# A mixed MLP and segment-attention kernel on one core: V computed first, transposes moved to DMA, speculation spread through the MLP, attention in a hand-set TensorE order

## The chip, the cores and the metric

One core of one Trainium2 chip. The metric is the device time of one execution in microseconds, the median of several runs. The kernel before took 1676.1 us here (4 runs, 1675.5 to 1676.5).

## The reference, cut to what matters

```python
def reference(...):                                  # bf16 inputs, S = 2048 tokens, D = 1024
    xn = layernorm(A_x)
    return A_x + A(xn) + B(xn)

def A(x):                                            # 64 segments of 32 tokens, 32 heads of 128
    mem = mem0                                       # 8 rows
    for s in range(64):
        h = concat([mem, x[segment s]])              # 40 rows
        q, k, v = h @ Wq, h @ Wk, h @ Wv             # 1024 -> 4096 each
        p = softmax(where(mask, q @ k.T * scale, -1e9))
        o = (p @ v) @ Wo
        mem = o[:8];  outs.append(o[8:])

def B(x):                                            # token-shift MLP
    h  = gelu(layernorm(x) @ w1)                     # 1024 -> 1024
    x1 = x + shift(h) @ w2                           # four channel groups shifted by -1, +1, -2, +2 tokens
    return x1 + gelu(layernorm(x1) @ w3) @ w4        # 1024 -> 3584 -> 1024
```

The recurrence over `mem` is broken by speculation: both kernels guess every segment's memory rows from averages (71 rows in all), run all segments in parallel with the guesses, and verify them at the end. If the check fails, a serial fallback runs.

## The kernel before: the parts that matter

The stages are: first stage (normalise the tokens, transpose them, `w1`, GELU), stage two (`w2`, residual, second norm, transpose), the MLP (`w3`, GELU, `w4`, four token blocks of 512), the speculation in one piece before the last `w4` chain, then attention in blocks of 12 segments with the output projection after each block. A scheduler decides the order of instructions on each engine.

```python
# first stage, for each of 16 token tiles: 8 identity matmuls for xn2, 8 "spread" matmuls for xn
nc.tensor.matmul(ps[:, k, :], xn2[:, (k0 + k) * P:(k0 + k + 1) * P], ident[:], start=True, stop=True)
nc.tensor.matmul(ps[:, k, :], xn[:, (k0 + k) * P:(k0 + k + 1) * P], spread[:], start=True, stop=True)   # 132 columns
...
# attention, for each block and each of 8 groups of 4 heads
for B, QT in zip(Bs, QTs):
    proj_T(B, wq, QT, QSCALE)            # 32 matmuls, 396 columns
for B, KTt in zip(Bs, KTs):
    proj_T(B, wk, KTt, None)             # 32 matmuls, 396 columns
for B, V in zip(Bs, Vs):
    proj_V(B, wv, V, cs_)                # 24 matmuls of 512 columns, then small DMAs put V in place
for B, QT, KTt, V in zip(Bs, QTs, KTs, Vs):
    attention(B, hg, QT, KTt, V)
...
# inside attention(): one tile = 3 segments with their memory rows, T = 99 rows, 4 heads at once
nc.tensor.matmul(S3[:, hh, :], QT[:, hh, l0:l0 + T], KTt[:, hh, l0:l0 + T], start=True, stop=True)      # scores
nc.vector.tensor_tensor(sm[:T, :, :T], S3, msk..., op=ALU.add)
nc.vector.tensor_reduce(mx[:T, :], sm[:T, :, :T], axis=AX.X, op=ALU.max)
nc.vector.tensor_tensor(sm[:T, :, :T], sm[:T, :, :T], mx..., op=ALU.subtract)
nc.scalar.activation(e[:T, :, :T], sm[:T, :, :T], ACTF.Exp, scale=LN2)
nc.vector.tensor_reduce(ss[:T, :], e[:T, :, :T], axis=AX.X, op=ALU.add)
nc.vector.reciprocal(rs[:T, :], ss[:T, :])
nc.vector.tensor_tensor(Pn[:T, :, :T], e[:T, :, :T], rs..., op=ALU.mult)
nc.tensor.matmul(T3[:, hh, :], Pn[:T, hh, :T], ident[:T, :T], start=True, stop=True)                    # transpose
nc.scalar.copy(PT[:T, :, :T], T3)
nc.tensor.matmul(O3[:, hh, :], V[:T, ti, hh * P:(hh + 1) * P], PT[:T, hh, :T], start=True, stop=True)   # outputs
...
# memory rows: 71 rows are the stationary side, 512 columns move (speculation, their V, verification)
nc.tensor.matmul(psz[ch][:NQ, :], vbT[:, h, :], wo[:, hh, ch * 512:(ch + 1) * 512], ...)
```

## Time and profile before

The page of the kernel before: its span, the busy time of the engines, and, in 40 equal slices of the span, the busy share of TensorE (PE) and the clock granted to it, in tenths. PEld are TensorE's weight loads, DVE is VectorE, ACT ScalarE, POOL GpSimd; SP, further down, is SyncE, which issues most of the DMAs here.

```profile
span 1674.9 us, 26877 instructions
PE 1626.2 (97%) x10393; PEld 863.9 (52%) x10513; DVE 647.2 (39%) x1528; ACT 640.6 (38%) x1321; POOL 220.9 (13%) x380
PE   6999999999999999999999999999999999999998
PEclk9999999999999999999999999999999999999999
```

TensorE is busy nearly always and at full clock, while every other engine is idle for more than half the time. Busy time alone does not say whether TensorE could be faster: matmuls are pipelined, so the cost of one is better read from start to start. In steady state these steps were 216 ns for 512 columns, 168 for 396, 58 for 132, 56 for 128, 47 for 99 and 35 for 71. Multiplied by the counts in the program they give a **floor**: the time that TensorE would need if it never waited. For this kernel it is 1572 us. The other 103 us I call the excess.

Four of the eleven lines of the list of TensorE's waits of the kernel before (what waited, for what: us in total, times, longest):

```profile
PE ps L233 <- ACT xn_160 L223: 10.9, 1, 10.9
PE ps L241 <- DVE xn2T L235: 5.4, 2, 4.3
PE psT L483 <- DVE Pn L479: 4.3, 14, 0.9
PE ps L147 <- DMA wv<-in_A_Wv_dram: 2.6, 3, 1.4
```

It holds few long waits after the start. The rest of the excess is in small pieces. The timeline of TensorE inside attention (start, duration, line, tiles, count) shows them:

```profile
1018.80 0.33 PE L419 MATMUL ps<-hTb,wk 128*128 128x396 bf16 x1
1019.10 0.34 PE L489 MATMUL psO<-PT,V_9567 99*128 99x99 bf16 x4
1019.43 0.39 PE L483 MATMUL psT<-c_ident_sb,Pn 99*99 99x99 bf16 x4
1019.66 1.01 PE L419 MATMUL ps<-hTb,wk 128*128 128x396 bf16 x5
1020.50 0.34 PE L489 MATMUL psO<-PT,V_9567 99*128 99x99 bf16 x4
```

Outputs (L489) and transposes (L483) stand one or two groups behind what they depend on, so many of them start 0.1 to 0.2 us late (in these rows the output at 1019.10 and the transpose at 1019.43). A group of heads takes 19.4 us against a floor of 18.1.

By stage (rows: window, its length, then busy time and instructions of PE, PEld, DVE, ACT and POOL, granted clock, DMA share, GB/s):

```profile
11.00:94.00 83.00, 76.16 (x634) 49.77 (x642) 45.16 (x122) 56.92 (x111) 22.98 (x36) 1.00 0.69 259
94.00:163.00 69.00, 64.44 (x361) 30.77 (x367) 48.66 (x107) 33.49 (x44) 21.22 (x32) 0.98 0.60 206
163.00:579.00 416.00, 410.81 (x2106) 191.99 (x2145) 32.92 (x61) 71.94 (x120) 39.26 (x31) 1.00 0.35 119
579.00:1669.00 1090.00, 1074.69 (x7295) 591.31 (x7360) 512.37 (x1215) 475.58 (x1045) 130.92 (x265) 1.00 0.49 151
```

The rows are the first stage, stage two, the MLP with the speculation, and attention with V.

### The profile page before, as it was taken

Reading aid. Unit: us, or ns where it says so; the run is one execution under the profiler, and the core shown is the slowest. Engines: PE = TensorE matmul, PEld = TensorE weight load, DVE = VectorE, ACT = ScalarE, POOL = GpSimd, SP = SyncE. Lnnn points to the kernel's source line nnn. Section 1 sums busy time; section 2 is a strip of 40 time slices with the busy share of each in tenths; the row PEclk is TensorE's granted clock in tenths of the full one; section 3 lists DMA queues with packets and bytes.
Section 4 is the critical chain, followed back from the end, with each engine's and each line's share of the span. In section 5 each row is a group of like instructions: output and inputs, shape, how many; then the busy total and the mean of one; then the engine's idle time right before and its main releaser. Section 6 shows DMA issues by size and latency. Waiting matters only on the chain.

```text
span 1674.9 us, 26877 instructions
## 1 busy us (share of the span) xinstructions
PE 1626.2 (97%) x10393; PEld 863.9 (52%) x10513; DVE 647.2 (39%) x1528; ACT 640.6 (38%) x1321; POOL 220.9 (13%) x380
## 2 busy tenths in 40 slices
PE   6999999999999999999999999999999999999998
PEld 5544444444445455554555545554555546665643
DVE  8447000000101145552455505564255533465540
ACT  7635302112030044541455415553255514565520
POOL 4222011010200122220111101110011100101000
PEclk9999999999999999999999999999999999999999
DMA  6864421030309887552565526564365633445211
GB/s 243 327 201 166 176 65 62 32 95 1 120 7 341 301 293 244 175 173 72 178 189 178 165 86 194 178 190 141 116 193 172 183 95 118 138 129 152 65 45 46
DMA packets 202804, 252.95 MB, mean 151 GB/s; under 512 B 15691, under 2 KB 165400, under 8 KB 202672
## 3 DMA queue, kind: packets, MB, share of 16 engines
q1 hardware_dynamic: 186928, 217.25, 41.1%
q0 software_dynamic: 15744, 33.92, 5.7%
q8 instruction: 85, 1.39, 0.3%
q14 instruction: 47, 0.39, 0.1%
HBM read 204.11 MB, written 30.07 MB: 140 GB/s over the span
## 4 chain that ended last, share of the span: by engine, by line
PE 75%; DVE 10%; ACT 5%; DMA 4%; issue 3%; POOL 0%; SPq 0%; DVEq 0%; ACTq 0%; POOLq 0%
PE ps L419 16%; PE ps L431 13%; PE ps L317 11%; PE ps L362 11%; PE ps L338 11%; DVE Pn L479 3%; DVE ss L475 2%; PE psT L483 2%; PE psO L489 2%; PE ps L256 2%; ACT e L473 2%; PE psS L466 2%; DMA wv<-in_A_Wv_dram 1%; DVE sm L471 1%; DVE sm L468 1%
## 5 line engine op out<-in xcount | busy, mean ns | idle before, releaser
L419 PE MATMUL ps<-hTb,wk 128*128 128x396 bf16 (+2 forms) x1536 | 265.7, 313 | 0.0
L419 PE MATMUL ps<-hTb,wq 128*128 128x396 bf16 (+2 forms) x1536 | 263.5, 314 | 0.8 <-DVE Ro L339 0.8
L362 PE MATMUL ps<-wo_sb,oX 128*128 128x512 bf16 x998 | 226.4, 379 | 1.2
L431 PE MATMUL ps<-wv,xTb 128*128 128x512 bf16 x984 | 224.4, 379 | 2.1
L338 PE MATMUL ps<-w_sb,h3T 128*128 128x512 bf16 x876 | 194.9, 379 | 1.1
L317 PE MATMUL ps<-xn3T,w_sb 128*128 128x512 bf16 x876 | 193.3, 379 | 1.1
L468 DVE TENSOR_TENSOR sm<-psS,c_mask_reg_sb 99x396 f32<-99x396 f32 x160 | 87.4, 563 | 218.1 <-PE psS L466 218.1
L419 PEld LDWEIGHTS <-wq 128*128 128x128 bf16 x1536 | 133.7, 98 | 71.3 <-issue 1.1
L318 ACT ACTIVATE h3T<-ps 128x512 bf16<-128x512 f32 x112 | 66.6, 597 | 268.1 <-PE ps L317 213.7
L419 PEld LDWEIGHTS <-wk 128*128 128x128 bf16 x1536 | 131.4, 98 | 67.5
L431 PEld LDWEIGHTS <-xTb 128*128 128x128 bf16 x1024 | 99.9, 98 | 115.7
L362 PEld LDWEIGHTS <-oX 128*128 128x128 bf16 x1024 | 97.9, 98 | 112.1 <-DVE oX L492 1.6
L317 PEld LDWEIGHTS <-w_sb 128*128 128x128 bf16 x896 | 87.6, 98 | 105.2
L338 PEld LDWEIGHTS <-h3T 128*128 128x128 bf16 x896 | 86.9, 98 | 103.1
L432 ACT CAST Vp<-ps 128x512 bf16<-128x512 f32 x128 | 74.9, 585 | 151.4 <-PE ps L431 146.8
L485 ACT CAST PT<-psT 99x396 bf16<-99x396 f32 (+1 forms) x176 | 85.9, 488 | 63.4 <-PE psT L483 61.3
L475 DVE TENSOR_REDUCE ss<-e 99x4 f32<-99x396 f32 (+1 forms) x176 | 95.0, 545 | 23.4 <-ACT e L473 22.3
L479 DVE TENSOR_TENSOR Pn<-e,rs 99x396 bf16<-99x396 f32 (+1 forms) x176 | 97.7, 559 | 6.9 <-DVE rs L477 0.5
L473 ACT ACTIVATE e<-sm 99x396 f32<-99x396 f32 (+1 forms) x176 | 90.4, 529 | 23.7 <-DVE sm L471 19.6
L490 ACT CAST oS<-psO 128x396 bf16<-128x396 f32 (+1 forms) x176 | 85.3, 485 | 33.4 <-PE psO L489 31.5
L471 DVE TENSOR_TENSOR sm<-sm,mx 99x396 f32<-99x396 f32 (+1 forms) x176 | 94.0, 553 | 0.5
L470 DVE TENSOR_REDUCE mx<-sm 99x4 f32<-99x396 f32 (+1 forms) x176 | 91.9, 541 | 1.1
(651 smaller groups left out, 1428.8 us busy)
## 6 DMA issues: line engine op xcount, KB each, us to landing
wv<-in_A_Wv_dram SPq DMA_DIRECT2D x48, 1024.0 KB
wq<-in_A_Wq_dram SPq DMA_DIRECT2D x40, 1024.0 KB
wk<-in_A_Wk_dram SPq DMA_DIRECT2D x40, 1024.0 KB
xt<-in_A_x_dram SPq DMA_DIRECT2D x32, 256.0 KB
R_scratch<-Ro POOLq DMA_DIRECT2D x16, 512.0 KB, 5.0
wo<-in_A_Wo_dram SPq DMA_DIRECT2D x8, 1024.0 KB
Rt<-R_scratch SPq DMA_DIRECT2D x32, 256.0 KB
wo_sb<-in_A_Wo_dram SPq DMA_DIRECT2D x4, 2048.0 KB
```

Of the source, the lines that this page charges most:

```text
L317: nc.tensor.matmul(ps[:], w3_sb[:, k, f * P:(f + 1) * P], xn3T[:, k, tb * 512:(tb + 1) * 512], start=(k == 0), stop=(k == KT - 1))
L338: nc.tensor.matmul(ps[:], h3T[:, f, j * P:(j + 1) * P], w4_sb[:, f, ch * 512:(ch + 1) * 512], start=(f == 0), stop=(f == FT - 1))
L362: nc.tensor.matmul(ps[:], oX[:, h, gl * P:(gl + 1) * P], wo_sb[:, h, cc], start=(h == 0), stop=(h == H - 1))
L419: nc.tensor.matmul(ps[:, :nb], w[:, k, hh * P:(hh + 1) * P], B["hTb"][:, k, :nb], start=(k == 0), stop=(k == KT - 1))
L431: nc.tensor.matmul(ps[:], B["xTb"][:, k, m * P:(m + 1) * P], wv[:, k, :], start=(k == 0), stop=(k == KT - 1))
L468: nc.vector.tensor_tensor(sm[:T, :, :T], S3, msk[:].unsqueeze(1).to_broadcast((T, 4, T)), op=ALU.add)
L470: nc.vector.tensor_reduce(mx[:T, :], sm[:T, :, :T], axis=AX.X, op=ALU.max)
L471: nc.vector.tensor_tensor(sm[:T, :, :T], sm[:T, :, :T], mx[:T, :].unsqueeze(2).to_broadcast((T, 4, T)), op=ALU.subtract)
L473: nc.scalar.activation(e[:T, :, :T], sm[:T, :, :T], ACTF.Exp, scale=LN2)
L475: nc.vector.tensor_reduce(ss[:T, :], e[:T, :, :T], axis=AX.X, op=ALU.add)
L479: nc.vector.tensor_tensor(Pn[:T, :, :T], e[:T, :, :T], rs[:T, :].unsqueeze(2).to_broadcast((T, 4, T)), op=ALU.mult)
L485: nc.scalar.copy(PT[:T, :, :T], T3)
```

## The change

Its intent: take off TensorE what need not be there, and stop it from waiting in attention.

- V for all tokens is computed in a stage of its own, written to DRAM, and read back tile by tile.
- Transposes become DMA transposes issued by SP: 12 of 16 token tiles in the first stage, all of stage two, the tokens for V and attention, and the probabilities of all 176 tile-and-head-group pairs.
- The speculation is cut into 25 units that sit between the chains of the MLP.
- The three products over the memory rows swap sides, so the 71 rows become the moving side.
- The maximum and its subtraction leave the softmax (a range check on the sums falls back if needed).
- The order on TensorE is set by hand: scores and outputs of a tile are placed between projection groups by a small clock model, outputs at least `LAT = 8` us after their scores; output projections are cut into pieces of four heads.

The diff, cut to its core:

```diff
+    with tc.manual_schedule(engines={mybir.EngineType.PE}), ExitStack() as actx:
 ...  first stage
-                            nc.tensor.matmul(ps[:, k, :], xn[...], spread[:], start=True, stop=True)
+                        if not on_pe:                                  # on_pe = n0 < 4
+                            nc.sync.dma_start_transpose(xn2T[:, jj], xn2[:])
+                            nc.tensor.matmul(ps[:, k, :], xn[:, k * P:(k + 1) * P], segsum[:], start=True, stop=True)  # 4 columns
 ...  stage two
-                            nc.tensor.matmul(ps[:, k, :], xn3[...], ident[:], start=True, stop=True)
+                        nc.sync.dma_start_transpose(xn3T[n // 4][:, n % 4], xn3[:])
 ...  MLP: the speculation's units
-                    speculate(psum, wpool, spool)
+                        if tb == 0 and f == 20:
+                            mem_start()
+                        if tb > 0 and f % 7 == 6:
+                            spec_step()
 ...
+                            if tb == 0 and j == 0 and ch == 0:
+                                spec_load()
+                            elif tb > 0 or j > 1:
+                                spec_step()
 ...  attention
-                nc.vector.tensor_reduce(mx[:T, :], sm[:T, :, :T], axis=AX.X, op=ALU.max)
-                nc.vector.tensor_tensor(sm[:T, :, :T], sm[:T, :, :T], mx..., op=ALU.subtract)
-                    nc.tensor.matmul(T3[:, hh, :], Pn[:T, hh, :T], ident[:T, :T], start=True, stop=True)
-                nc.scalar.copy(PT[:T, :, :T], T3)
+            nc.sync.dma_start_transpose(PTr, Pn[:rows].rearrange("p h k -> p (h k)"))
 ...  order
-                for B, QT, KTt, V in zip(Bs, QTs, KTs, Vs):
-                    attention(B, hg, QT, KTt, V)
+                            proj(B, w, hh, dst, scale)
+                            tick(8 * (B["nb"] / 2400 + 0.0025), blocked=...)   # emits the scores and outputs now due
+                        smalls.append((clock[0] + LAT, ("O", gi_), o_item))
```

## The prediction

> **What bounds the kernel now.** TensorE: the page gives PE 97% busy of 1674.9 us at full granted clock, DVE 39%, ACT 38%, DMA 151 GB/s. The list of waits shows about 30 us of PE waits, 10.9 before the first matmul. Start to start, matmuls took 216 ns for 512 columns, 168 for 396, 58 for 132, 56 for 128, 47 for 99, 35 for 71; times the counts in the program this is a floor of 1572 us. The other 103 us: 11 before the first matmul, 6 after the last, 13 in the first stage (to 94 us), about 60 in attention (from 579 us; in the timeline a head group takes 19.4 us against a floor of 18.1, as score, transpose and output matmuls stand just behind DVE and ACT), the rest in the MLP.
>
> **TensorE work removed** (same durations):
> - identity transposes of the probabilities, 704 matmuls: -33 us, now DMA transposes
> - transposes of normalised tokens: 128 became 32 in the first stage (-5), 128 became 0 after stage two (-7); spread matmuls became 4-column sums (-4)
> - three products for the memory rows: 64 matmuls of 216 ns become 256 of 35: -14
> - projections, V, MLP, output projection: same columns
>
> The instruction order confirms the counts; new floor 1507 us, 65 less.
>
> **Waits.** Speculation moves between MLP chains, which cover its loads (the 2.6 us wait for wv goes). PE order is fixed: 9.2 us of other matmuls stand between a tile's scores and its outputs. The chain between: mask add 0.56, exp 0.54, sum 0.56, reciprocal 0.17, product 0.57, with hops about 3 us (max and subtraction, 1.1 us, are gone), then one DMA transpose of about 110 KB, which has 6 us. No DMA transpose is in this trace; small DMAs issued by POOL landed in 5 to 6 us. The Trainium skill, "DMA: Bandwidth & Descriptors", section "Latency and other measured facts", gives transposes 261 GB/s in the worse layout; an estimate from it is under 0.5 us of transfer beside the fixed latency, so it should fit, with little to spare behind 1 MB weight loads in the same queue. DVE falls to near 30%. V goes through DRAM (16 MB written, read again); its stage has DMA to spare.
>
> **Sum (estimate).** Start 11 + first stage 61 + 10 + stage two 55 + 3 + MLP with speculation 414 + 6 + V 221 + 3 + attention with output projection and verification 755 + 25 + end 6 = 1570 us. All 65 us of removed matmuls are on the critical path, since PE is never idle for long; some 40 of the 103 us of excess go too.
>
> Predicted 1570 us, 8 in 10 between 1535 and 1625. Faster by over 2%: 0.93; within 2%: 0.05; slower: 0.02.
>
> **What would show it.** PE at 97% or more; no identity matmuls for probabilities; a head group of a block at 12.2 to 13 us without its V; waits of output matmuls for transposed probabilities under 10 us in total; V stage at 222 us; no PE gaps at the MLP-to-V and V-to-attention borders.
>
> **What would make it wrong.** A DMA transpose, queueing included, over 6 us: output matmuls wait and the loss repeats every third tile; 9 us would cost up to 25% of attention. SP issues in order, so a weight load waiting for its buffer can hold a transpose behind it. DMA transposes in the first stage could starve stage one by 10 to 20 us. Four-row strided moving operands might stream slower than 168 ns. A failed verification would run the serial fallback and cost milliseconds.

## The result

The changed kernel took **1609.5 us** (4 runs, 1595.8 to 1612.8) against 1676.1. The ratio is 0.9589, 95% interval 0.9550 to 0.9628. Here and below a ratio is the mean time of one kernel's fast runs over that of the other's of the same rounds, so it is not quite the ratio of the medians. In a second job it was 1606.4 us (5 runs, 1603.2 to 1606.6), ratio 0.9577 (0.9564 to 0.9590). So the change is faster by 4%, inside the predicted range, but by 67 to 70 us where 106 were forecast.

The page of the changed kernel:

```profile
span 1604.6 us, 25081 instructions
PE 1537.0 (96%) x10222; PEld 830.5 (52%) x10222; DVE 525.3 (33%) x1149; ACT 511.5 (32%) x1183; POOL 89.7 (6%) x114
PE   5799998999999999999999999999999999999998
PEclk9899999999999999999999999999999999999999
```

TensorE is still the limit, but at 96% of a shorter span, and with a visible dent in the first slices. Nine of the thirteen lines of its list of waits:

```profile
PE ps L247 <- ACT xn_152 L233: 13.4, 1, 13.4
PE psO L575 <- DMA PT<-Pn_6360: 10.1, 9, 2.1
PE ps L264 <- DMA xn2T<-xn_788: 8.2, 1, 8.2
PE ps L370 <- DMA wt<-in_A_Wv_dram: 5.2, 2, 3.9
PE ps L436 <- ACT h3T L437: 4.8, 1, 4.8
PE ps L264 <- DMA xn2T<-xn_474: 3.6, 1, 3.6
PE gps_3027 L384 <- DMA wot<-in_A_Wo_dram: 3.5, 2, 3.0
PE psO L575 <- DMA PT<-Pn_6359: 2.6, 3, 1.2
PE psO L575 <- DMA PT<-Pn_6361: 2.5, 4, 1.5
```

Nearly all of it is new: transposes of the first stage (L264), loads of the speculation (L370, L384), the first GELU of the MLP (L436), and outputs that wait for transposed probabilities (L575, 15.2 us over three buffers). In these rows of attention the small pieces are gone:

```profile
1009.68 2.87 PE L540 MATMUL ps<-hTb,wt 128*128 128x396 bf16 x16
1012.39 0.34 PE L575 MATMUL psO<-PT,V_8268 99*128 99x99 bf16 x4
1012.57 0.35 PE L551 MATMUL psS<-KT_8428,QT_8427 128*99 128x99 bf16 x4
1012.76 2.87 PE L540 MATMUL ps<-hTb,wt 128*128 128x396 bf16 x16
```

Four such rounds, a head group, take 12.5 us (V is made elsewhere). The stages, as before, with V in a row of its own (the fourth) and attention in the fifth:

```profile
13.00:96.00 83.00, 68.79 (x600) 47.67 (x601) 35.27 (x117) 40.93 (x76) 20.06 (x30) 0.92 0.81 232
96.00:151.00 55.00, 55.00 (x263) 25.07 (x262) 45.32 (x101) 17.10 (x15) 20.12 (x30) 1.00 1.04 292
151.00:588.00 437.00, 423.42 (x2577) 204.52 (x2576) 42.05 (x89) 69.90 (x115) 41.48 (x35) 0.98 0.50 148
588.00:810.00 222.00, 221.12 (x1026) 100.16 (x1025) 44.94 (x66) 37.41 (x64) 1.99 (x4) 1.00 0.45 150
810.00:1599.00 789.00, 768.51 (x5763) 453.07 (x5761) 351.42 (x762) 343.92 (x913) 0.00 (x0) 1.00 0.69 170
```

The first stage does 9 us less work in the same 83 us, at a mean clock of 0.92. The MLP has 4 us more to do than before (the speculation's products included) and takes 20 us longer.

The table takes the profiled execution apart: the excess of a stage is its length (from its first matmul to the next stage's) less the floor of its matmuls.

| us | before: length | excess | predicted: length | excess | after: length | excess |
|---|---|---|---|---|---|---|
| to the first matmul | 10.9 | 10.9 | 11 | 11 | 13.4 | 13.4 |
| first stage | 82.9 | 13.0 | 71 | 10 | 83.0 | 22.3 |
| stage two | 69.3 | 6.8 | 58 | 3 | 55.2 | 0 |
| MLP and speculation | 416.3 | 6.0 | 420 | 6 | 435.9 | 21.5 |
| V and attention | 1089.3 | 60.2 | 1004 | 27 | 1011.3 | 34.0 |
| after the last matmul's start | 6.2 | 6.2 | 6 | 6 | 5.8 | 5.8 |
| sum | 1674.9 | 103 | 1570 | 63 | 1604.6 | 97 |

The floor fell from 1572 to 1507 us as forecast. The excess did not fall by 40 us, but by 6: attention and stage two gained 33 us, and the first stage, the MLP and the start gave 27 back.

### A wait costs more than its length

After the longer waits TensorE runs at half clock for some microseconds. Around the wait of 4.8 us in the MLP (window, length, PE busy, granted clock, DMA share, GB/s; this view is of TensorE alone):

```profile
152.00:158.30 6.30, 6.30 (x31) 1.00 1.17 264
158.30:163.60 5.30, 0.45 (x4) 0.85 0.85 182
163.60:168.90 5.30, 5.30 (x13) 0.50 0.84 287
168.90:174.20 5.30, 5.30 (x26) 1.00 1.02 389
```

In the 5.3 us after the wait 13 matmuls ran where 26 run at full clock. So this wait cost 4.8 us and then another 2.7. The same follows the speculation waits at 261 and 371 us and both first-stage waits: after these five waits, 23.5 us together, TensorE worked 26.5 us at half clock, which is a loss of some 13 us. Over the whole execution the recorded half-clock stretches last 41.7 us, against 7.6 before; 4.2 us of each lie after the last matmul and cost nothing. The records begin at 20.8 us (before) and 22.1 us (after); until then both kernels run slow as well (107 ns from start to start for 128 columns). The Trainium skill, "TensorE: Matmul & The Clock Gate", section "Part 1: The HAM clock gate", says that the clock falls to half after an idle window of about 3.4 us, and that windows are 3413 ns long. On the length the trace agrees: up to the last matmul the stretches of this run last 3.413, 6.827 or 10.24 us. On what starts them it does not quite agree (see the last section). The prediction costed every wait at its length alone.

### The profile page after: what moved, and what is told of

Same layout as the page of the kernel before. It is cut to its first block, busy times and chain, and to the rows that moved or that the text cites. A ratio compares the mean times of both kernels' runs of the same rounds, so it can differ in the third digit from the quotient of the medians.

```text
span 1604.6 us, 25081 instructions
## 1 busy us (share of the span) xinstructions
PE 1537.0 (96%) x10222; PEld 830.5 (52%) x10222; DVE 525.3 (33%) x1149; ACT 511.5 (32%) x1183; POOL 89.7 (6%) x114
## 3 DMA queue, kind: packets, MB, share of 16 engines
q1 hardware_dynamic: 333888, 249.23, 58.2%
## 4 chain that ended last, share of the span: by engine, by line
PE 73%; DMA 9%; DVE 1%; issue 1%; ACT 0%; POOL 0%; SPq 0%; ACTq 0%; POOLq 0%
PE ps L540 23%; PE pso L593 14%; PE ps L481 14%; PE ps L436 9%; PE ps L460 8%; DMA PT<-Pn_6360 3%; PE psO L575 2%; PE psS L551 2%; DMA PT<-Pn_6361 2%; DMA PT<-Pn_6359 1%; DMA hTb<-xn_scratch 1%; PE ps L693 1%; DMA R_scratch<-R_3128 1%; PE ps L404 1%; DMA wot<-in_A_Wo_dram 1%
## 5 line engine op out<-in xcount | busy, mean ns | idle before, releaser
L540 PE MATMUL ps<-hTb,wt 128*128 128x396 bf16 (+1 forms) x2560 | 403.7, 311 | 0.0
L540 PEld LDWEIGHTS <-wt 128*128 128x128 bf16 x3072 | 272.0, 98 | 167.3 <-issue 4.5
L481 PE MATMUL ps<-wt,xT 128*128 128x512 bf16 x1024 | 221.2, 379 | 0.0
L481 PEld LDWEIGHTS <-xT 128*128 128x128 bf16 x1024 | 100.2, 98 | 120.8
L436 PEld LDWEIGHTS <-w_sb 128*128 128x128 bf16 x896 | 88.1, 99 | 112.3 <-issue 11.4
L557 DVE TENSOR_REDUCE sums<-sm 99x4 f32<-99x396 f32 (+1 forms) x176 | 97.6, 554 | 117.6 <-ACT sm L555 117.5
L555 ACT ACTIVATE sm<-sm 99x396 f32<-99x396 f32 (+1 forms) x176 | 92.8, 527 | 54.0 <-DVE sm L553 49.8
L540 PE MATMUL ps<-hTb_5138,wt 128*128 128x403 bf16 x512 | 93.6, 335 | 2.4 <-ACT QT_6369 L544 1.5
L264 PE MATMUL ps<-xn2T,w_sb 128*128 128x256 bf16 (+2 forms) x448 | 65.9, 309 | 13.8 <-DMA xn2T<-xn_788 8.2
L601 DVE TENSOR_TENSOR ot<-pso,Rt 128x512 bf16<-128x512 f32 x32 | 22.1, 691 | 156.1 <-PE pso L593 152.8
L264 PEld LDWEIGHTS <-w_sb 128*128 128x128 bf16 x448 | 41.0, 106 | 32.7 <-issue 9.8
L436 PE MATMUL ps<-xn3T_1209,w_sb 128*128 128x512 bf16 x224 | 51.4, 393 | 4.8 <-ACT h3T L437 4.8
L315 PE MATMUL ps<-w_sb,hTB 128*128 128x512 bf16 x256 | 55.4, 379 | 0.0
L436 PE MATMUL ps<-xn3T_1210,w_sb 128*128 128x512 bf16 x224 | 51.0, 390 | 0.0
L436 PE MATMUL ps<-xn3T_1211,w_sb 128*128 128x512 bf16 x224 | 49.0, 379 | 0.0
L436 PE MATMUL ps<-xn3T_1212,w_sb 128*128 128x512 bf16 x224 | 48.5, 379 | 0.0
```

The lines of the kernel that those rows point to most:

```text
L264: nc.tensor.matmul(ps[:, :w].rearrange("p (n t) -> p n t", t=P), w1_sb[:, k, co * P:(co + 1) * P], xn2T[:, :nt, k, :], start=(k == 0), sto ...
L315: nc.tensor.matmul(ps[:], hTB[:, k, o:o + P], w2_sb[:, k, ch * 512:(ch + 1) * 512], start=(k == 0), stop=(k == KT - 1))
L436: nc.tensor.matmul(ps[:].rearrange("p (n t) -> p n t", t=P), w3_sb[:, k, f * P:(f + 1) * P], xn3T[tb][:, :, k, :], start=(k == 0), stop=(k ...
L481: nc.tensor.matmul(ps[:], xT[:, m4 * 4 + j, k, :], wv[:, k, :], start=(k == 0), stop=(k == KT - 1))
L540: nc.tensor.matmul(ps[:, :nb] if B["b"] in (0, 5) else ps[:, :nb].rearrange("p (t c) -> p t c", t=4), w[:, k, hh * P:(hh + 1) * P], B["rhs ...
L557: nc.vector.tensor_reduce(ss, e[:T, :, :T], axis=AX.X, op=ALU.add)
```

## The experiments

Each was timed against the kernel before, in the same job. The changed kernel is 0.9577 to 0.9589 of it; 0.001 is 1.7 us. Stage lengths are those of the profiled execution.

### The changed kernel again

No edit.

> The changed kernel again, to know its spread: its first four runs lay between 1596 and 1613 us, and the longer ones had the lower mean granted clock. Expected 1595 to 1613 again, mean ratio to the kernel before 0.957 to 0.961, and a longer run has a lower clock in the records.

Measured: 1606.4 us (1603.2 to 1606.6), ratio 0.9577. Two runs with a mean clock of 0.992 took 1603.2 and 1604.0 us, three with 0.990 took 1606.4 to 1606.6. The spread agrees in direction with more or less half clock, though that does not show what starts it. In this repeat the waits of the MLP were much the same (5.0, 4.4 and 3.2 us), but the half clock after the two speculation waits lasted one stretch of 3.4 us instead of two, and TensorE worked 20.6 us at half clock in all instead of 29.9. So the loss at half clock, some 10 us here and 15 there, changes without any edit.

### First-stage transposes back on TensorE

```diff
-                        on_pe = n0 < 4
+                        on_pe = n0 < 16
-                            todo = trs + todo
+                            todo = todo + trs
```

> All 16 transposes of the first stage back on TensorE (96 matmuls of 56 ns, +5.4 us, and 24 evictions on DVE and ACT), segment sums moved ahead of them in the PE order so that the rings do not lock. Theory A, the DMA transposes of the first stage come late and cost 12 us of PE waits plus some 6 us of half clock after them: the first stage ends 8 to 14 us earlier (at about 84 us instead of 96) and the whole is 1596 to 1602 us. Rival, the first stage is bound by DVE, ACT or the loads of x and the transposes only show it: the waits move to DVE or ACT, the first stage ends at 93 us or later, and the whole stays within 4 us of 1609.

Measured: 1598.1 us (1596.7 to 1604.7), ratio 0.9538 (0.9521 to 0.9554). The total is what theory A named, but not for its reason. The first stage took 80.4 us instead of 83.0 and ended at 94.1: the waits for DMA went, and TensorE waited for the evictions (copies of results out of PSUM) on DVE and ACT instead, as the rival said. The largest of these in its list:

```profile
PE ps L264 <- DVE xn2T L249: 3.6, 4, 1.8
```

The stage's matmuls grew by 5.4 us and its excess fell by 8, so here the DMA transposes cost more than the columns that they saved. Half clock fell from 41.7 to 15.5 us in all. So shorter, scattered waits replaced two long ones; about 3 of the 7 to 9 us lie in the first stage of the profiled run. The rest lies in stages that the edit does not touch: there the half clock after each of the three waits of the MLP lasted one stretch of 3.4 us instead of two, worth some 4 us, and the one in attention did not come, worth 1.7. The repeat above shows the same in part without any edit, so that the edit caused it is not shown.

### w3 loads held back

```diff
+                        if n == 15:
+                            last_xn2.append(a_xn2)
...
-                nc.sync.dma_start(w3_sb[:, :, c * 512:(c + 1) * 512], ...)
+                late = nc.sync.dma_start(w3_sb[:, :, c * 512:(c + 1) * 512], ...)
+                tc.add_manual_dep(late.ins, last_xn2[0].ins.name, ...)
```

> The seven 1 MB loads of w3 are held until the last token tile is normalised; nothing else changes. Theory A1, the transposes land late because bulk loads keep the DMA engines full in front of them: the two waits for xn2T (3.6 and 8.2 us) fall under 4 us together, the half clock in the first stage goes, total 1593 to 1600 us. Rival A2, the transposes themselves are slow (issue 1.2 to 5 us each on SP, 256-byte packets) and the ring of three sources holds ACT: the waits stay above 8 us and the total stays within 4 us of 1609.

Measured: 1599.3 us (1592.3 to 1607.9), ratio 0.9527 (0.9509 to 0.9546). The waits for `xn2T` fell from 11.8 to 3.0 us and the first stage from 83.0 to 72.9 us. In the changed kernel w3 loads were issued at 22.6, 23.1, 34.5, 44.2, 44.7, 57.0 and 64.4 us, among the transposes. Those transposes needed 3.2 to 9.0 us from the start of their issue to the last completion mark, 5.0 at the median; in this run the same twelve needed 3.1 to 5.8, 3.4 at the median. So A1 holds and A2 falls. But w3 now came in a burst (69.5 to 89.6 us) in front of stage two's reloads of `xn`: stage two grew from 55.2 to 64.4 us, and TensorE waited 9.9 us instead of 4.8 for the first GELU of the MLP.

```profile
PE ps L268 <- DMA xn2T<-xn: 3.0, 2, 2.6
PE ps L442 <- ACT h3T L443: 9.9, 1, 9.9
```

In the profiled execution all of the gain was handed on. It is the slowest of the five (1607.9 us), so it does not explain the better median.

### h3T placed elsewhere, twice

```diff
+                h3T = big.tile([P, FT, 512], BF16)
                 w4_sb = big.tile([P, FT, D], BF16)
-                h3T = big.tile([P, FT, 512], BF16)
```

> h3T is allocated ahead of w4, so it lies over hTB (free when stage two's matmuls end) and no longer over the rows that the last transpose of stage two reads. Theory: ACT's first GELU of the MLP waited for that transpose to land (4.4 us), PE ran out of PSUM banks behind it and then ran 5.6 us at half clock: the wait at 158 us and the half clock after it both go, 7 to 8 us less (about 1602). Rival for the half clock: it does not follow from the wait, then 5 us less and a half-clock stretch near 165 us remains.

Measured: 1603.6 us (1602.4 to 1607.2), ratio 0.9561 (0.9549 to 0.9573). The theory fell: the wait shrank only from 4.8 to 3.6 us. The list of ACT's waits of this run, from 145 to 185 us, still has the last transpose of stage two in it:

```profile
ACT h3T L437 <- DMA xn3T<-xn: 3.0, 1, 3.0
```

In its timeline four engines go on within 0.2 us of each other when that transpose has landed: DVE at 162.58, ACT at 162.62, SP at 162.63 and POOL at 162.76 us, SP with loads of w4. That suggests that whatever lies in the new pool waits for everything that the closed pool of stage two held, wherever `h3T` stands. So the second try gave it a pool that opens before stage two:

```diff
+            h3_pool = bctx.enter_context(tc.tile_pool(name="h3", bufs=1))
+            h3T = h3_pool.tile([P, FT, 512], BF16)
             with ExitStack() as hctx:
...
-                h3T = big.tile([P, FT, 512], BF16)
```

> h3T in a pool of its own, opened before stage two, so no wait is inherited from the pool that stage two closes (in the run that only swapped h3T and w4 the first GELU still waited 3.0 us for the last transpose). Theory, the wait belongs to the whole closed pool: the first GELU waits for its matmuls alone, the 3.6 to 5 us of PE wait and the half clock after it go, MLP 427 to 430 us instead of 432 to 436, total 5 to 8 us less than the changed kernel in the same rounds. Rival, the MLP only moves the time into its next wait: total within 3 us.

Measured: 1597.0 us (1589.5 to 1598.7) against 1606.4 of the changed kernel in the same rounds, ratio to before 0.9521. The wait of the first GELU is gone, and the MLP took 424.2 us instead of 432.6. It is not a clean test, though: the pool also moved `w3_sb` onto memory that stage two's pools hold, so the w3 loads went out at 88 to 140 us, the first stage fell to 72.3 us and stage two grew to 65.7, as in the run with w3 held back. Against the repeat in the same rounds (84.0 and 58.2 us) the first two stages together gained 4 us as well. The 8 us of the MLP are of the size that 4.4 us of wait there, and its half clock, had.

### R1 and x loads on POOL

```diff
-                        nc.sync.dma_start(R1[:], R1_v[:, n, :])
+                        nc.gpsimd.dma_start(R1[:], R1_v[:, n, :])
-                        nc.sync.dma_start(xt[:], x_v[:, n, :])
+                        nc.gpsimd.dma_start(xt[:], x_v[:, n, :])
```

> The loads of the residual rows R1 and x in the MLP are issued by POOL instead of SP. Theory: SP issues in order, and an x load that waited for POOL held the next speculation weight load for 4 us after its buffer was free: the PE waits for wv and wo (8.7 us together) fall under 2 us, and with them two stretches of half clock (2.8 us each), total 1597 to 1602. Rival: with one free weight buffer a 1 MB load cannot arrive within the 6 us between two speculation steps, whoever issues: waits stay above 6 us, total within 4 us of 1609.

The reason to suspect the order on SP stands in the changed kernel's timeline. SP issues the x load (L455) once POOL is done with its buffer, and right after it the weight load (L364):

```profile
253.61 0.33 SPq L453 DMA_DIRECT2D R_2992<-R_scratch  x1
259.34 0.33 SPq L455 DMA_DIRECT2D xt<-in_A_x_dram  x1
259.77 7.98 SPq L364 DMA_DIRECT2D wt<-in_A_Wv_dram  x2
```

```profile
254.03 1.29 PE L370 MATMUL ps<-xb,wt 128*128 128x71 bf16 x32 [1.33 <-DMA wt<-in_A_Wv_dram]
265.24 2.10 PE L370 MATMUL ps<-xb,wt 128*128 128x71 bf16 x32 [3.88 <-DMA wt<-in_A_Wv_dram]
```

The weight buffer was free at 255.3, when the previous unit's matmuls ended; its load left at 259.8, and the next unit waited 3.9 us for it. Measured with the loads on POOL: 1597.4 us (1589.7 to 1606.6), ratio 0.9523 (0.9492 to 0.9555). The waits for `wv` and `wo` fell from 8.7 to 0.8 us and the MLP from 435.9 to 421.7; of their lines this one is left:

```profile
PE ps L370 <- DMA wt<-in_A_Wv_dram: 0.8, 1, 0.8
```

The theory holds: it was the place in the queue, not the speed of the load.

### Outputs farther behind the scores

```diff
-        LAT = 8.0
+        LAT = 11.0
-            PT = smp.tile([P, 4, 112], BF16, tag="PT", bufs=5)
+            PT = smp.tile([P, 4, 112], BF16, tag="PT", bufs=6)
```

> PE order alone: outputs stand 12.1 us of other matmuls behind their scores instead of 9.2 (median over the tiles), with six buffers for the transposed probabilities instead of five. In the changed kernel the chain to the probabilities takes 3.0 us and the transpose 4.6 us from issue to landing (median), 6.2 at the ninth decile, so about a tenth of the tiles come late. Theory: the 15 to 18 us of PE waits for transposed probabilities fall under 4 us, attention (789 us) becomes 770 to 777 us, total about 1594 to 1600. Rival: the transposes are late because SP holds them behind other issues or because the DMA engines are full, so they stay late whatever the distance: waits stay above 10 us, total within 4 us of 1609.

Measured: 1586.6 us (1581.2 to 1591.3), ratio 0.9468 (0.9448 to 0.9488). Attention took 771.0 us instead of 789.2, and no wait for a transposed probability is left in the list. The total beat the expectation by 7 us; in the profiled execution 4.5 us of the gain lie in the MLP, which the edit does not touch. At the ninth decile the transposes were as slow as before (6.2 us in both; the median fell from 4.6 to 3.7), so it is the distance that took the waits away. The sixth buffer was not tried without the distance.

### Outputs closer to the scores

```diff
-        LAT = 8.0
+        LAT = 5.0
```

> The other way: outputs only 6.1 us of matmuls behind their scores. Theory: nearly every tile waits 1.5 us or more, and as two tiles are under way at a time the loss repeats every second tile: attention grows by 60 to 140 us, total 1670 to 1750, which would take the whole gain away. Rival: what is late is only a few tiles behind weight loads, then attention grows by under 20 us.

Measured: 1699.5 us (1696.2 to 1702.2), ratio 1.0138 (1.0122 to 1.0154), slower than the kernel before by 1.4%. Attention took 889.6 us, 100 more. The first line of its list of waits:

```profile
PE psO L575 <- DMA PT<-Pn: 90.2, 61, 4.3
```

The theory had nearly every tile wait; 61 waits in 176 tiles are enough. They are 75 us more than in the changed kernel, and TensorE worked 42 us of attention at half clock instead of 3.4, which lost some 19 more. One constant in the order, 3 us, is worth more than the whole change.

### Transposes of the probabilities back on TensorE

```diff
-            nc.sync.dma_start_transpose(PTr, Pn[:rows].rearrange("p h k -> p (h k)"))
+                nc.tensor.matmul(T3[:, hh, :], Pn[:T, hh, :T], ident[:T, :T], start=True, stop=True)
+            nc.scalar.copy(PTr[:T, :, :T], T3)          # placed 5 us behind the scores, outputs at 8 us as before
-        ps = apsum.tile([P, 512], F32, tag="mm", bufs=4)
+        ps = apsum.tile([P, 512], F32, tag="mm", bufs=3)
-        head, rest = outs[:4], outs[4:]
+        head, rest = outs[:3], outs[3:]
```

> Transposes of the probabilities back on TensorE (704 matmuls of 47 ns, evicted by ACT, one PSUM bank taken from the projections), at a fixed place 5 us after the scores; all else as changed. Theory: the columns are worth their full 33 us, less the 15 us of waits for transposes that go: attention 805 to 815 us, total 1625 to 1635. Rival: TensorE had slack there and the transposes cost nothing: total within 6 us of 1609.

Measured: 1623.7 us (1622.4 to 1628.6), ratio 0.9697 (0.9681 to 0.9713); attention 809.4 us, 20.2 more than the changed kernel. The 15.2 us of waits for DMA transposes went, so the columns cost 20.2 + 15.2 = 35 us where the floor says 33 (an estimate: one PSUM buffer less and the new places in the order came with them). The expectation's total (1625 to 1635) was missed by 1 us. The columns are worth what was counted, and in the changed kernel almost half of it is paid back as waits.

### One part of the change in the kernel before

```diff
-                nc.vector.tensor_reduce(mx[:T, :], sm[:T, :, :T], axis=AX.X, op=ALU.max)
-                nc.vector.tensor_tensor(sm[:T, :, :T], sm[:T, :, :T], mx..., op=ALU.subtract)
```

> The kernel before with one part of the change alone: no maximum and no subtraction in the softmax (1.1 us less of DVE per tile, 340 instructions). Theory: DVE is off the critical path (39% busy) and the scheduler puts the dependent matmuls just as close behind the shorter chain, so less than 12 us goes of the 60 us that attention has above its floor, total 1664 to 1676. Rival: the short waits in attention are due to that chain's length, then 20 us or more go, total 1655 or less.

Measured: 1659.8 us (1658.5 to 1660.6), ratio 0.9901 (0.9886 to 0.9916); attention 1071.1 us instead of 1089.3. Neither theory: 16 us, between the two. DVE was 39% busy, and yet shortening its chain took 18 of attention's 60 us of excess. A likely reason is that matmuls stand so close behind the chain that its length shows; the run does not prove that. The other 42 us did not go with it.

### Four mends together

The POOL loads, `LAT = 11` and the pool for `h3T` as above, and the w3 loads in step with their use:

```diff
+                gate = gates[0] if c < 2 else gates[min(c - 1, len(gates) - 1)]   # last norm, then stage two's tiles
+                tc.add_manual_dep(late.ins, gate.ins.name, ...)
```

> Four mends at once: w3 loads gated (two chunks after the last norm, the rest one per token tile late in stage two), h3T in a pool of its own opened before stage two so that GELU waits for nothing of stage two, R1 and x loads on POOL, and outputs 12.1 us behind scores. Theory: the losses are separate and their mends add: first stage 83 to 73 us, stage two 55 to 60, MLP 436 to 416, attention 789 to 773, total 1565 to 1578, half clock under 15 us in all. Rival: they share one cause (DMA engines full), the mends push the wait along: total 1585 or more.

Measured: 1573.2 us (1570.5 to 1575.6), ratio 0.9391 (0.9378 to 0.9404). First stage 71.6 us, stage two 55.3, attention 771.3, each as expected or better; the MLP, at 428.7, was not, and half clock lasted 21.8 us. One line of its waits says why:

```profile
PE ps L364 <- DMA m<-in_A_mem_dram: 12.5, 1, 12.5
```

SP issues the 16 KB load of the memory rows after all of w4 (at 174.2 us), and its first product stood too early in TensorE's order. In every run of the changed kernel without the pool for `h3T` that load left at 96 to 100 us, in the three with it at 171 to 182: that mend moved it.

### And the memory rows' product moved

```diff
-                        if tb == 0 and f == 20:
-                            mem_start()
...
                             if tb == 0 and j == 0 and ch == 0:
+                                mem_start()
                                 spec_load()
```

> As the run with four mends, and the memory rows' first product moved from the first GELU chain of the MLP to just before the first speculation load, since there PE waited 12.7 us for the 16 KB load of the memory rows, which SP issued after all of w4, and ran at half clock after it. Theory: that wait and its half clock (2 us) go and nothing takes their place: MLP 429 to 415 us, total 1556 to 1562. Rival: the load is late there too, or the next load of the speculation is: total above 1566.

Measured: **1558.3 us** (1556.2 to 1561.8), ratio 0.9295 (0.9282 to 0.9308), correct. This beats both kernels. Its busy line and the two longest waits in its list:

```profile
PE 1522.0 (98%) x10222; PEld 827.0 (53%) x10222; DVE 523.5 (34%) x1149; ACT 508.4 (33%) x1183; POOL 106.3 (7%) x146
PE ps L253 <- ACT xn L237: 13.6, 1, 13.6
PE psO L583 <- ACT oT_m L586: 2.9, 5, 0.7
```

After the start no kind of wait adds up to 3 us. The stages are 72.7, 57.2, 416.6, 222.1 and 771.9 us, half clock lasts 11.5 us, and the excess is 53 us (1560.1 of the profiled run less 1507). So with the same matmuls as the changed kernel, the forecast 63 us of excess was reachable.

## Why the prediction was right or wrong

- **"TensorE" bounds the kernel; "new floor 1507 us, 65 less"; "All 65 us of removed matmuls are on the critical path".** Right. The time fell by 67 to 70 us; putting the largest item back cost 35 us, waits counted, where 33 were reckoned. Of the other items only the first-stage transposes were put back (5.4 us), and there waits hid the columns. That the whole fell by little more than the floor is partly luck: 33 us of excess were gained and 27 lost.
- **"a head group of a block at 12.2 to 13 us"; "V stage at 222 us"; no gap from the MLP to V.** Right: 12.5 and 222.1 us, no gap. At the border from V to attention, where none was predicted either, two waits of 0.9 and 1.5 us came.
- **"PE at 97% or more".** Wrong: 96%.
- **"some 40 of the 103 us of excess go too".** This is the term that was mis-sized: it was 6 (103 to 97), so the excess came out 34 us above the forecast 63. Its parts:
  - **"Speculation moves between MLP chains, which cover its loads".** Wrong. They waited 8.7 us, and half clock followed. The cause was neither bandwidth nor the size of the chains but the place on SP behind x loads, as the run with POOL loads showed (MLP 14 us shorter). The prediction named this head-of-line hazard, but only for the probabilities.
  - **"first stage 61 + 10".** Excess 22 instead of 10. The risk was named ("could starve stage one by 10 to 20 us"), but left out of the sum. Transposes queued among bulk loads of w3 caused it: with w3 held back the stage took 72.9 us.
  - **The MLP's "+ 6".** Besides the loads there was a wait that the diff does not show: the first GELU inherits the end of stage two's pool through its last DMA transpose.
  - **"waits of output matmuls for transposed probabilities under 10 us in total".** Wrong: 15.2 us. The chain of 3.0 us was right to the decimal; the transpose, for which 6 us were left, took 4.6 us at the median but 6.2 at the ninth decile. The warning about what a longer one would cost was right in kind: taking 3 us of distance away cost 100 us.
  - **Half clock** was not in the prediction at all. Every wait was costed at its length alone, while TensorE worked 29.9 us at half clock, a loss of some 15 us.

What stays open: whether the edit itself shortened the half clock outside the first stage when the transposes went back to TensorE, and how the 9 us of the mended first GELU split between the wait itself and the displaced w3 loads. No run tests the hand-set order, the V stage or the swapped memory products alone.

## What to carry to other kernels

Count the columns that a change takes off TensorE, since they came true to 2 us of 33; then look at what each DMA that replaces them must share a queue with, and set the distance for its ninth decile, not its median. In this kernel a wait of several microseconds on TensorE cost about half as much again, since the clock was halved after it (five waits of 23.5 us, then some 13). When an excess has several causes, mend one at a time and look at the stage after it: here holding w3 back handed its 10 us on to the next stage, and only the loads in step with their use, in the run of four mends, kept both stages short (71.6 and 55.3 us).

## What the Trainium skill lacked or had wrong

- "DMA: Bandwidth & Descriptors", section "Latency and other measured facts": it gives a transpose 261 GB/s, and 350 to 400 in the contiguous case. The 16 transposes of 256 KB for the V stage took SP mostly 1.31 us each to issue, one after the other, which is a pace of 200 GB/s (262,144 bytes in 1.31 us). Whether SP or the DMA engines (share 0.95 from 539 to 561 us) set that pace is not shown. SP's time for a transpose (1.19 us at the median for 112 x 512 elements, against 0.40 for a plain load of 1 MB) belongs in a plan as well.
- The same page, section "Rules for kernel authors", says that a transpose next to ordinary DMAs needs nothing. All results here were correct, so it holds for that, but not for time: the twelve 256 KB transposes of the first stage landed 3.2 to 9.0 us after the start of their issue among the loads of w3, and 3.1 to 5.8 us after it with these held back. No page that I read gives a landing time under load.
- "TensorE: Matmul & The Clock Gate", section "Part 1: The HAM clock gate", gives an idle window of about 3.4 us as the trigger. Here half clock also came after shorter waits: a stretch of 3.4 us at 1414.7 us of the changed kernel, after waits of 0.7, 0.2 and 1.0 us within the 3.2 us before it, and in the run with h3T ahead of w4 one at 927.7 us after a wait of 1.9 us. The longest such wait of the changed kernel, 2.1 us, had none.
